# Channel loop of a gated attention and state-space kernel: the state recurrences of two neighbouring blocks overlapped by half

## The chip, the cores and the metric

The kernel runs on one core of one Trainium2 chip. The metric is the device time of one execution in microseconds (us); lower is better. The kernel before takes 2762.11 us (median of 3 runs, 2752.1 to 2769.66).

## The reference, cut to what matters

The reference computes a gated mix of two branches over a sequence of 2048 positions and 576 channels, and the gradients of it for twelve inputs. Branch A is multi-head attention with 32 heads of 18. Branch B is a state-space convolution with 128 complex states per channel:

```
logdA = dt * (A_re + 1j*A_im);  dB = dt * (B_re + 1j*B_im)
P = exp(logdA[:, :, None] * l)                  # channels x 128 states x 2048
K = einsum("dn,dnl,dn->dl", Cc, P, dB).real     # one filter of 2048 taps per channel
y = irfft(rfft(u) * rfft(K))[:L] + u * Dskip    # a causal convolution per channel
out = g * a + (1 - g) * b
```

The kernel does not form the filter. It cuts the sequence into 16 blocks of 128 positions (NB) and carries the 128 complex states of a channel from block to block: a recurrence of the form H[k] = Z * H[k-1] + U[k], with the complex number Z a constant of channel and state. The forward pass (call it h, s = 0 in the code) and the gradient (g, s = 1) are the same recurrence on two inputs, so a channel has four real rows: real and imaginary part of h and of g. There are NS = 15 states in sequence, that is one start value and 14 steps.

## The kernel before, in words

Three stages follow one another. Attention and its gradient take the first 2107 us or so. The channel loop is next, and it is the stage that changes. A last stage forms the weight gradients and the two outputs.

The channel loop goes over 18 blocks of 32 channels (NBLK = 18, CB = 32). The 128 states lie on the partitions. The work of block b is spread over several iterations, and these helpers do it:

- `load_en(b, h)` (L671) loads half h of the block's basis, E1n, 1 MB, from device memory. Six halves fit, so block b takes the place of block b-3, after `ybp(b-3, h)` has read it. `turn_e` (L654) transposes one half on TensorE (32 matmuls, etp) and copies it out on ScalarE (4 copies, E1e, L665).
- `m_load(b)` (L603) loads xs, 1 MB, and gyp; `m_part` (L610) multiplies them on TensorE (psM, 16 matmuls per call), copies the sum on ScalarE (mst, L620) and stores it (Md_d). `m_skw` (L628) reads Md_d back along a skewed pattern in four loads (skw), and `m_sum` and `m_fin` turn that into two more columns of RX.
- `prep_rx` (L590) makes the matmul input RX in three ScalarE instructions (L597 to L599), from RXn, which `load_rx` loads for two blocks at a time.
- `uv(b, h)` (L676) makes the inputs of the recurrence for half h: 32 matmuls (uvp) and 4 ScalarE evictions (UV, L690).
- `scan(b, 0, 15)` (L692) is the recurrence, on VectorE. A step is two chains, h and g, each of three instructions: a product of the last state with Z and with its swapped partner (tz, L704, 128x128), the addition of the input (L706, 128x64), and the sum of both products (HG, L708, 128x64). The chains alternate, so an instruction never depends on the one right before it.
- `casts` (L710), on ScalarE, makes bf16 copies hR and gR of the states. `rw1` and `rw2` (L719, L726), on VectorE, weight the states for the output. `ybp` (L756) multiplies them with E1n on TensorE (64 matmuls). `pairs1` and `pairs2` (L786, L793) multiply states with inputs on VectorE (pq, L774 and L802), and TensorE sums them (59 matmuls, misc); `sums` copies the sums out (m, L808).
- `k0(b)` (L732) computes tap 0 of the block's filter in 65 narrow matmuls, copies it (K0c, L744) and stores it; `t0_load` (L813) then loads T0w, 1 MB, the Toeplitz block made of the stored taps, and `t0` multiplies with it (32 matmuls).

The order is written out by hand for TensorE, ScalarE, VectorE and GpSimd: each engine runs its instructions in program order. Only the order of DMA issues on SyncE inside the loop is left to the framework's scheduler. All loads and stores of the loop are issued by SyncE into one hardware queue. The PSUM tiles etp, uvp and psM share one ring of four banks (tag "bk").

Of one iteration i before, this is the order: `k0(i+1)`, `uv(i+1, 0)`, `turn_e(i+1, 1)`, `scan(i)`, `casts(i)`, `rw1`, `rw2`, `t0(i)`, `uv(i+1, 1)`, `prep_rx(i+2)`, `ybp(i)`, `pairs1(i)`, `load_en(i+3)`, `turn_e(i+2, 0)`, `m_sum` and `m_fin(i+2)`, `pairs2(i)`, `sums(i)`, `m_part(i+3)`. So what block i+2 needs from the first half of its basis is made at the end of iteration i, and the rest in iteration i+1, beside the recurrence of block i.

Of the kernel before, what the change touches and what calls it, by code (L numbers as in the profile page):

```python
# [9 lines left out]
A = mybir.AluOpType  # L10
ACT = mybir.ActivationFunctionType
BF = mybir.dt.bfloat16
F32 = mybir.dt.float32
# [7 lines left out]
def build(tc, aps, dbg_aps=None, stages=("s1", "attn", "post", "s4", "final")):  # L21
# [40 lines left out]
    with ExitStack() as gctx:  # L62
# [538 lines left out]
        xss = {}  # L601

        def m_load(b, dma=nc.sync.dma_start):  # L603
            xs = xss[b] = Q["pl"].tile([P, NSUB, SUB, CB], BF, tag="xs", bufs=2, name="xs")
            src = bass.AP(tensor=xb_d.tensor, offset=xb_d[b:b + 1, 0:1, 0:1].offset,
                          ap=[[XR * SUB * CB, NB], [SUB * CB, NSUB], [1, NSUB * SUB * CB]])
            dma(xs.rearrange("p e t c -> p (e t c)"), src)
            dma(Q["gyp2"][b % 2][:, 0:SUB, :].rearrange("p t c -> p (t c)"), gyb_d[b])
# [56 lines left out]
                copy(E_[:, 4 * q:4 * q + 4], pt_)  # L665

        def load_par(b, dma=nc.sync.dma_start):
            par = blk(b)["par"] = Q["pw"].tile([P, 8, CB], F32, tag="par", bufs=2, name="par")
            dma(par, par_d[:, 0:8, b * CB:(b + 1) * CB])

        def load_en(b, h, dma=nc.sync.dma_start):  # L671
            dG = b * CB + h * GS
# [3 lines left out]
        def uv(b, h):  # L676
            B_ = blk(b)
            if h == 0:
                B_["UV"] = Q["pw"].tile([P, 2, NCOL, CB], BF, tag="UV", bufs=2, name="UV")
            UV = B_["UV"]  # L680
            E_ = B_["E"].pop(h)
            RX = RXs[b // 2][1]
            off = (b % 2) * CB + h * GS
            for q in range(2):
                for ri in range(2):
                    pr = Q["ps"].tile([P, NCOL, 8], F32, tag="bk", bufs=4, name="uvp")
                    for c_ in range(8):
                        mm(pr[:, :, c_], lhsT=E_[:, q * 8 + c_, ri, :], rhs=RX[:, off + q * 8 + c_, :])
                    c0 = h * GS + q * 8
                    nc.scalar.mul(UV[:, ri, :, c0:c0 + 8], pr, -1.0 if ri == 0 else 1.0)  # L690

        def scan(b, k0, k1):  # L692
            B_ = blk(b)
            UVk = B_["UV"][:, :, 0:2 * NB, :].rearrange("p r (s k) c -> p r s k c", s=2)
            if k0 == 0:
                B_["HG"] = Q["pw"].tile([P, 4, NS, CB], F32, tag="HG", name="HG")
                nc.vector.tensor_copy(B_["HG"][:, :, 0, :].rearrange("p (r s) c -> p r s c", s=2), UVk[:, :, :, 0, :])
                k0 = 1
            HG = B_["HG"].rearrange("p (r s) k c -> p s r k c", s=2)
            ZZ = B_["par"][:, 0:4, :].rearrange("p (m r) c -> p m r c", m=2)  # L700
            for k in range(k0, k1):
                tz = [Q["pw"].tile([P, 2, 2, CB], F32, tag=f"tz{s_}", bufs=2, name="tz") for s_ in range(2)]
                for s_ in range(2):
                    nc.vector.tensor_tensor(tz[s_], HG[:, s_, :, k - 1, :].unsqueeze(1).to_broadcast([P, 2, 2, CB]), ZZ, op=A.mult)  # L704
                for s_ in range(2):
                    nc.vector.tensor_tensor(tz[s_][:, 0], tz[s_][:, 0], UVk[:, :, s_, k, :], op=A.add)  # L706
                for s_ in range(2):
                    nc.vector.tensor_tensor(HG[:, s_, :, k, :], tz[s_][:, 0], tz[s_][:, 1, ::-1], op=A.add)  # L708

        def casts(b):  # L710
            B_ = blk(b)
# [6 lines left out]

        def rw1(b):  # L719
            B_ = blk(b)  # L720
            for nm, r_, tg in (("wa", 4, "wA"), ("wb", 5, "wB")):
                B_[nm] = Q["pw"].tile([P, 4 * NS, CB], F32, tag=tg, name=nm)
                nc.vector.tensor_tensor(B_[nm], B_["HG"].rearrange("p q k c -> p (q k) c"),
                                        B_["par"][:, r_, :].unsqueeze(1).to_broadcast([P, 4 * NS, CB]), op=A.mult)
# [7 lines left out]
        def k0(b):  # L732

            B_ = blk(b)
            wk = Q["pw"].tile([P, 2, CB], BF, tag="wk", bufs=2, name="wk")
            nc.scalar.copy(wk, B_["par"][:, 6:8, :])
            kps = Q["misc2"][b % 2][:, 13 * CB:14 * CB]
            mm(kps, lhsT=ident_bf[0:1, :], rhs=Q["dsk_row"][:, b * CB:(b + 1) * CB], start=True, stop=False)
            for ch in range(CB):
                for ri in range(2):  # L740
                    mm(kps[:, ch:ch + 1], lhsT=B_["En"][ch // GS][:, ch % GS, ri, :], rhs=wk[:, ri, ch:ch + 1],
                       start=False, stop=(ch == CB - 1 and ri == 1))
            K0c = Q["pw"].tile([P, CB], BF, tag="K0c", bufs=2, name="K0c")
            nc.scalar.copy(K0c, kps)  # L744
            nc.sync.dma_start(Kp_d[b, P:2 * P, :], K0c)
# [67 lines left out]
        def t0_load(b):  # L813
            B_ = blk(b)
            if "T0w" in B_:
                return
            T0w = B_["T0w"] = Q["pw"].tile([P, P, CB], BF, tag="T0w", bufs=2, name="T0w")
            src = bass.AP(tensor=Kp_d.tensor, offset=Kp_d[b:b + 1, 1:2, 0:1].offset, ap=[[CB, P], [1, P * CB]])
            nc.sync.dma_start(T0w.rearrange("p j c -> p (j c)"), src)

# [476 lines left out]
        if "s4" in stages:  # L1297
# [8 lines left out]
            with ExitStack() as ctx:  # L1306
# [24 lines left out]

                ctx.enter_context(tc.manual_schedule(engines={mybir.EngineType.PE, mybir.EngineType.Activation, mybir.EngineType.DVE, mybir.EngineType.Pool}))
                dve_copy = nc.vector.tensor_copy
                with tc.manual_schedule(engines={mybir.EngineType.SP}):
                    load_par(0)
                    prep_rx(0, dve_copy)
                    turn_e(0, 0, 0, 4, dve_copy)
                    m_sum(0)
                    m_fin(0)
                    uv(0, 0)  # L1340
                    turn_e(0, 1, 0, 4, dve_copy)
                    uv(0, 1)
                    m_skw(1)
                    load_en(2, 0)
                    load_par(1)
                    prep_rx(1)
                    k0(0)
                    t0_load(0)
                    turn_e(1, 0, 0, 4)
                    m_load(2)  # L1350
                    m_sum(1)
                    m_fin(1)
                    load_en(2, 1)
                for i in range(NBLK):
                    cur = True
                    nx = i + 1 < NBLK
                    mb = i + 3 if i + 3 < NBLK else None
                    sb = i + 2 if i + 2 < NBLK else None
                    if sb is not None and i > 0:
                        m_skw(sb)  # L1360
                    if sb is not None:
                        load_par(sb)
                    if mb is not None:
                        m_load(mb)
                    if sb is not None and sb % 2 == 0:
                        load_rx(sb // 2)
                    if nx and cur:
                        k0(i + 1)
                    if nx:
                        uv(i + 1, 0)  # L1370
                        turn_e(i + 1, 1, 0, 4)
                    if cur:
                        scan(i, 0, 15)
                        casts(i)
                        rw1(i)
                        rw2(i)
                        t0(i, 0)
                        t0(i, 1)
                    if nx:
                        uv(i + 1, 1)  # L1380
                    if sb is not None:
                        prep_rx(sb)
                    if i == 0:
                        m_part(2, 0)
                        m_part(2, 1)
                        m_skw(2)
                    if cur:
                        if nx:
                            t0_load(i + 1)
                        ybp(i, 0)  # L1390
                        ybp(i, 1)
                        pairs1(i)
                    if cur and mb is not None:
                        load_en(mb, 0)
                        load_en(mb, 1)
                    if sb is not None:
                        turn_e(sb, 0, 0, 4)
                        m_sum(sb)
                        m_fin(sb)
                    if cur:  # L1400
                        pairs2(i)
                        sums(i)
                    if mb is not None:
                        m_part(mb, 0)
                        m_part(mb, 1)
                    if cur:
                        BK.pop(i)

        while rights:
            rights.pop().__exit__(None, None, None)  # L1410
# [295 lines left out]
```

## Time and profile before

| what | value |
|---|---|
| median of 3 runs | 2762.11 us (2752.1 to 2769.66) |
| the profiled execution | 2755.74 us, its span 2754.0 us |
| TensorE / VectorE / ScalarE busy over the span | 88% / 85% / 86% |
| mean granted TensorE clock | 0.954 |
| first instruction of the first recurrence (HG, L697) | 2119.04 us |
| last sum of the last block on TensorE ends | 2584.50 us |
| recurrence instructions (L704, L706, L708) | 3 x 504 |

The shares over the whole span say little about the loop, since attention fills three quarters of it. The loop is read from the stretch 2119 to 2585 us: the busy time of each engine in windows of 50 us, the groups of instructions there, and one iteration of about 25 us in order of time. A start-to-start distance of two instructions on one engine is what an instruction costs in a queue; its listed duration is longer, since the end of one overlaps the start of the next.

### The profile page before, as it was taken

How to read it: one execution, taken by the hardware profiler on the slowest of the kernel's cores; microseconds unless marked ns; L12 is line 12 of the kernel's file. 1: busy time of each engine (PE TensorE's matmuls, PEld its weight loads, DVE VectorE, ACT ScalarE, POOL GpSimd, SP SyncE). 2: the span in 40 equal slices, each digit the busy share in tenths (PEclk: the TensorE clock that was granted, in tenths of full speed). 3: DMA queues.
4: the chain of work that ended last, by engine and by line, in shares of the span. 5: the costliest groups of instructions: out<-in, count | busy, mean ns of one | idle time of the engine just before them, and what ended most of it. 6: DMA issues, size and time to landing. Idle time of an engine off the chain costs nothing.

```text
span 2754.0 us, 70696 instructions
## 1 busy us (share of the span) xinstructions
PE 2429.9 (88%) x27411; PEld 1170.9 (43%) x27411; DVE 2348.6 (85%) x4850; ACT 2368.6 (86%) x2749; POOL 1611.9 (59%) x2667
## 2 busy tenths in 40 slices
PE   8798989988989988889999889988885899999789
PEld 4433333333333333333333333333323788888557
DVE  5649999999999998899999989998985899999954
ACT  5489999999999999999999999999974788888221
POOL 0278878888988888788888878888501000000010
PEclk9889999999999999999999999999977899899899
DMA  7637899889888978987997898797779898986995
GB/s 226 182 102 157 150 169 179 160 159 190 158 159 175 173 159 165 176 161 157 175 161 163 160 172 162 152 186 151 138 156 204 228 257 219 246 238 167 254 244 137
DMA packets 1256763, 490.81 MB, mean 178 GB/s; under 512 B 1151781, under 2 KB 1228182, under 8 KB 1247210
## 3 DMA queue, kind: packets, MB, share of 16 engines
q1 hardware_dynamic: 1219946, 413.78, 73.2%
q0 software_dynamic: 23120, 59.76, 8.8%
q10 hardware_dynamic: 13360, 12.75, 1.6%
q8 instruction: 214, 3.51, 0.5%
q14 instruction: 123, 1.01, 0.1%
HBM read 145.68 MB, written 98.52 MB: 89 GB/s over the span
## 4 chain that ended last, share of the span: by engine, by line
ACT 38%; PE 26%; DVE 23%; issue 6%; DMA 4%; POOL 2%; SPq 1%; ACTq 0%; DVEq 0%; POOLq 0%
ACT eb L1271 22%; ACT PT L1266 14%; DVE ds L1276 7%; PE ps_P L30 7%; DVE tz L704 3%; PE accV L30 2%; PE ps_dx L30 2%; PE turn_p L988 2%; DVE tz L706 2%; DVE HG L708 2%; PE accK L30 1%; PE ps_dwq L30 1%; DVE pq L774 1%; PE misc L30 1%; DMA dsT<-ds 1%
## 5 line engine op out<-in xcount | busy, mean ns | idle before, releaser
L1276 DVE TENSOR_TENSOR ds<-ps_P,PT 128x512 bf16<-128x512 f32 x2048 | 1312.6, 684 | 135.2 <-PE ps_P L30 97.5
L1271 ACT ACTIVATE eb<-ps_P 128x1024 bf16<-128x1024 f32 x1024 | 1100.8, 1075 | 31.1 <-PE ps_P L30 31.1
L1266 ACT ACTIVATE PT<-ps_P 128x1024 bf16<-128x1024 f32 x1024 | 1105.8, 1081 | 20.9 <-PE ps_P L30 19.6
L30 PE MATMUL ps_P<-dOaT,VaT_g 32*128 32x512 bf16 x2048 | 580.9, 388 | 31.1 <-DVE ds L1276 15.6
L502 POOL TENSOR_TENSOR et<-eG,eT 128x448 f32<-128x448 f32 x576 | 542.2, 961 | 10.7
L30 PE MATMUL ps_P<-QaT_g,KaT_g 32*128 32x512 bf16 x2048 | 402.0, 385 | 137.3 <-ACT PT L1266 122.8
L30 PE MATMUL ps_P<-KaT_g,QaT_g 32*128 32x512 bf16 x2048 | 406.1, 389 | 2.5 <-ACT eb L1271 1.9
L30 PEld LDWEIGHTS <-KaT_g 32*128 32x128 bf16 x2048 | 147.6, 91 | 467.3 <-issue 451.3
L502 POOL TENSOR_TENSOR Eo<-et,et 128x448 bf16<-128x448 f32 x288 | 326.9, 1135 | 20.7
L810 POOL TENSOR_TENSOR SS<-m 128x96 f32<-128x96 f32 x18 | 9.7, 537 | 429.5 <-ACT m L808 384.5
L30 PEld LDWEIGHTS <-QaT_g 32*128 32x128 bf16 x2048 | 116.0, 91 | 286.3 <-issue 263.9
L30 PE MATMUL accV<-eb,dOa 128*32 128x512 bf16 x2048 | 184.5, 393 | 27.5 <-ACT eb L1271 27.2
L30 PE MATMUL accO<-PT,Vtok_g 128*32 128x512 bf16 x2048 | 206.9, 393 | 0.1
L30 PE MATMUL accK<-dsT,Qtok_g 128*32 128x256 bf16 x4096 | 163.0, 280 | 14.8 <-DMA dsT<-ds 13.0
L30 PE MATMUL accQ<-ds,Ktok_g 128*32 128x512 bf16 x2048 | 160.3, 391 | 2.3 <-DVE dvacc L1042 2.2
L30 PEld LDWEIGHTS <-Vtok_g 128*32 128x32 bf16 x2048 | 52.7, 93 | 222.0 <-issue 222.0
L993 DVE COPY dsT<-turn_p 128x1024 bf16<-128x1024 bf16 (+1 forms) x216 | 139.3, 645 | 2.3 <-PE turn_p L988 2.3
L988 PE MATMUL turn_p<-ident_bf,ds 128*128 128x128 bf16 x1664 | 133.8, 223 | 1.6 <-DVE gb L1060 0.8
L665 ACT COPY E1e<-etp 128x1024 bf16<-128x1024 bf16 x136 | 128.8, 1060 | 3.4 <-PE etp L664 3.3
L704 DVE TENSOR_TENSOR tz<-HG,par 128x128 f32<-128x128 f32 x504 | 126.7, 295 | 0.6
L502 POOL TENSOR_TENSOR et<-eT 128x32 f32<-128x32 f32 (+3 forms) x288 | 115.8, 422 | 11.4
L30 PEld LDWEIGHTS <-Qtok_g 128*32 128x32 bf16 x4096 | 88.4, 97 | 77.7 <-issue 60.5
(264 smaller groups left out, 3692.5 us busy)
## 6 DMA issues: line engine op xcount, KB each, us to landing
E_d<-Eo POOLq DMA_DIRECT2D x144, 256.0 KB, 3.3
E1n<-E_d SPq DMA_DIRECT2D x36, 1024.0 KB
xs<-xb_d SPq DMA_DIRECT2D x18, 1024.0 KB
T0w<-Kp_d SPq DMA_DIRECT2D x18, 1024.0 KB
Md_d<-mst SPq DMA_DIRECT2D x36, 288.0 KB
dsT<-ds SPq DMA_TRANSPOSE x512
dqkv_d<-dtk POOLq DMA_DIRECT2D x96, 72.0 KB, 4.3
skw<-Md_d SPq DMA_DIRECT2D x72, 64.0 KB
```

Of the source, the lines that this page charges most:

```text
L30: return nc.tensor.matmul(out, lhsT=lhsT, rhs=rhs, start=start, stop=stop, **kw)
L502: nc.gpsimd.tensor_tensor(out, a, b, op=op)
L665: copy(E_[:, 4 * q:4 * q + 4], pt_)
L704: nc.vector.tensor_tensor(tz[s_], HG[:, s_, :, k - 1, :].unsqueeze(1).to_broadcast([P, 2, 2, CB]), ZZ, op=A.mult)
L706: nc.vector.tensor_tensor(tz[s_][:, 0], tz[s_][:, 0], UVk[:, :, s_, k, :], op=A.add)
L708: nc.vector.tensor_tensor(HG[:, s_, :, k, :], tz[s_][:, 0], tz[s_][:, 1, ::-1], op=A.add)
L774: nc.vector.tensor_tensor(o.rearrange("p a b n c -> p a b (n c)"), a_.rearrange("p b n c -> p b (n c)").unsqueeze(1).to_broadcast([P, 2, 2 ...
L988: nc.tensor.transpose(pt_[:, x, qb, :], t_[:, qb * P:(qb + 1) * P], ident_bf)
L993: (nc.scalar.copy if NTOT <= now[0] < NTOT + OFF else nc.vector.tensor_copy)(o_(), pt_[:, x:x + n])
L1266: nc.scalar.activation(U["PT"][i, j // 2], ps, ACT.Exp)
L1271: nc.scalar.activation(e, ps, ACT.Exp)
L1276: nc.vector.tensor_tensor(U["ds"][i][:, j, :], ps, U["PT"][i, j // 2][:, j % 2, :], op=A.mult)
```

## The change

The recurrence of block i+1 is started half an iteration before that of block i is done. KH = 8. In iteration i one call of `scan` runs steps 8 to 14 of block i and steps 1 to 7 of block i+1 as two alternating chains. A chain now handles h and g together: its instructions are twice as wide (tz 128x256, the additions and sums 128x128), and there are half as many. Only the first half of block 0 (ahead of the loop) and the second half of block 17 still split h from g.

For that, Z has to lie in the parameters twice, so `load_par` issues three DMAs in place of one and reads four of the eight rows twice. UV(i+2) must be complete one iteration earlier than before. So in iteration i both `turn_e` and both `uv` of block i+2 are done, and `m_part(i+3)`, `m_skw(i+3)`, `prep_rx(i+3)` come ahead of `ybp(i)`. `t0` stands first in an iteration, then `k0(i+1)`. The loop before the first iteration grows by the work that moved forward.

Buffers: UV gets three and HG two; xs and T0w, 1 MB each, have one instead of two.

```diff
@@ -601,7 +601,7 @@
         xss = {}
 
         def m_load(b, dma=nc.sync.dma_start):
-            xs = xss[b] = Q["pl"].tile([P, NSUB, SUB, CB], BF, tag="xs", bufs=2, name="xs")
+            xs = xss[b] = Q["pl"].tile([P, NSUB, SUB, CB], BF, tag="xs", bufs=1, name="xs")
             src = bass.AP(tensor=xb_d.tensor, offset=xb_d[b:b + 1, 0:1, 0:1].offset,
                           ap=[[XR * SUB * CB, NB], [SUB * CB, NSUB], [1, NSUB * SUB * CB]])
             dma(xs.rearrange("p e t c -> p (e t c)"), src)
@@ -665,8 +665,10 @@
                 copy(E_[:, 4 * q:4 * q + 4], pt_)
 
         def load_par(b, dma=nc.sync.dma_start):
-            par = blk(b)["par"] = Q["pw"].tile([P, 8, CB], F32, tag="par", bufs=2, name="par")
-            dma(par, par_d[:, 0:8, b * CB:(b + 1) * CB])
+            par = blk(b)["par"] = Q["pw"].tile([P, 12, CB], F32, tag="par", bufs=2, name="par")
+            for s_ in range(2):
+                dma(par[:, s_:8:2, :], par_d[:, 0:4, b * CB:(b + 1) * CB])
+            dma(par[:, 8:12, :], par_d[:, 4:8, b * CB:(b + 1) * CB])
 
         def load_en(b, h, dma=nc.sync.dma_start):
             dG = b * CB + h * GS
@@ -676,7 +678,7 @@
         def uv(b, h):
             B_ = blk(b)
             if h == 0:
-                B_["UV"] = Q["pw"].tile([P, 2, NCOL, CB], BF, tag="UV", bufs=2, name="UV")
+                B_["UV"] = Q["pw"].tile([P, 2, NCOL, CB], BF, tag="UV", bufs=3, name="UV")
             UV = B_["UV"]
             E_ = B_["E"].pop(h)
             RX = RXs[b // 2][1]
@@ -689,23 +691,36 @@
                     c0 = h * GS + q * 8
                     nc.scalar.mul(UV[:, ri, :, c0:c0 + 8], pr, -1.0 if ri == 0 else 1.0)
 
-        def scan(b, k0, k1):
+        def scan_open(b):
             B_ = blk(b)
-            UVk = B_["UV"][:, :, 0:2 * NB, :].rearrange("p r (s k) c -> p r s k c", s=2)
-            if k0 == 0:
-                B_["HG"] = Q["pw"].tile([P, 4, NS, CB], F32, tag="HG", name="HG")
-                nc.vector.tensor_copy(B_["HG"][:, :, 0, :].rearrange("p (r s) c -> p r s c", s=2), UVk[:, :, :, 0, :])
-                k0 = 1
-            HG = B_["HG"].rearrange("p (r s) k c -> p s r k c", s=2)
-            ZZ = B_["par"][:, 0:4, :].rearrange("p (m r) c -> p m r c", m=2)
-            for k in range(k0, k1):
-                tz = [Q["pw"].tile([P, 2, 2, CB], F32, tag=f"tz{s_}", bufs=2, name="tz") for s_ in range(2)]
-                for s_ in range(2):
-                    nc.vector.tensor_tensor(tz[s_], HG[:, s_, :, k - 1, :].unsqueeze(1).to_broadcast([P, 2, 2, CB]), ZZ, op=A.mult)
-                for s_ in range(2):
-                    nc.vector.tensor_tensor(tz[s_][:, 0], tz[s_][:, 0], UVk[:, :, s_, k, :], op=A.add)
-                for s_ in range(2):
-                    nc.vector.tensor_tensor(HG[:, s_, :, k, :], tz[s_][:, 0], tz[s_][:, 1, ::-1], op=A.add)
+            HG = B_["HG"] = Q["pw"].tile([P, 4, NS, CB], F32, tag="HG", bufs=2, name="HG")
+            UVk = B_["UVk"] = B_["UV"][:, :, 0:2 * NB, :].rearrange("p r (s k) c -> p r s k c", s=2)
+            nc.vector.tensor_copy(HG[:, :, 0, :].rearrange("p (r s) c -> p r s c", s=2), UVk[:, :, :, 0, :])
+
+        def scan(*chains):
+
+            def part(b, s_):
+                B_ = blk(b)
+                HG, ZZ = B_["HG"], B_["par"][:, 0:8, :].rearrange("p (m q) c -> p m q c", m=2)
+                if s_ is None:
+                    return HG, ZZ, B_["UVk"], 4
+                return HG[:, s_::2], ZZ[:, :, s_::2], B_["UVk"][:, :, s_:s_ + 1], 2
+
+            todo_ = []
+            for x, (b, k0, k1, s_) in enumerate(chains):
+                todo_.append((x, part(b, s_), k0, k1))
+            for t in range(max(k1 - k0 for _, _, k0, k1 in todo_)):
+                live = [(x, p_, k0 + t) for x, p_, k0, k1 in todo_ if k0 + t < k1]
+                tz = {}
+                for x, (HG, ZZ, UVk, n), k in live:
+                    tz[x] = Q["pw"].tile([P, 2, 4, CB], F32, tag=f"tz{x}", bufs=2, name="tz")[:, :, 0:n]
+                    nc.vector.tensor_tensor(tz[x], HG[:, :, k - 1, :].unsqueeze(1).to_broadcast([P, 2, n, CB]), ZZ, op=A.mult)
+                for x, (HG, ZZ, UVk, n), k in live:
+                    t0v = tz[x][:, 0].rearrange("p (r s) c -> p r s c", r=2)
+                    nc.vector.tensor_tensor(t0v, t0v, UVk[:, :, :, k, :], op=A.add)
+                for x, (HG, ZZ, UVk, n), k in live:
+                    t0v, t1v = [tz[x][:, m].rearrange("p (r s) c -> p r s c", r=2) for m in range(2)]
+                    nc.vector.tensor_tensor(HG[:, :, k, :].rearrange("p (r s) c -> p r s c", r=2), t0v, t1v[:, ::-1], op=A.add)
 
         def casts(b):
             B_ = blk(b)
@@ -814,7 +829,7 @@
             B_ = blk(b)
             if "T0w" in B_:
                 return
-            T0w = B_["T0w"] = Q["pw"].tile([P, P, CB], BF, tag="T0w", bufs=2, name="T0w")
+            T0w = B_["T0w"] = Q["pw"].tile([P, P, CB], BF, tag="T0w", bufs=1, name="T0w")
             src = bass.AP(tensor=Kp_d.tensor, offset=Kp_d[b:b + 1, 1:2, 0:1].offset, ap=[[CB, P], [1, P * CB]])
             nc.sync.dma_start(T0w.rearrange("p j c -> p (j c)"), src)
 
@@ -1331,6 +1346,7 @@
 
                 ctx.enter_context(tc.manual_schedule(engines={mybir.EngineType.PE, mybir.EngineType.Activation, mybir.EngineType.DVE, mybir.EngineType.Pool}))
                 dve_copy = nc.vector.tensor_copy
+                KH = NS // 2 + 1
                 with tc.manual_schedule(engines={mybir.EngineType.SP}):
                     load_par(0)
                     prep_rx(0, dve_copy)
@@ -1341,70 +1357,72 @@
                     turn_e(0, 1, 0, 4, dve_copy)
                     uv(0, 1)
                     m_skw(1)
-                    load_en(2, 0)
+                    m_load(2)
                     load_par(1)
                     prep_rx(1)
+                    scan_open(0)
+                    scan((0, 1, KH, 0), (0, 1, KH, 1))
+                    load_rx(1)
+                    turn_e(1, 0, 0, 4)
+                    m_sum(1)
+                    m_fin(1)
+                    uv(1, 0)
+                    load_en(2, 0)
                     k0(0)
                     t0_load(0)
-                    turn_e(1, 0, 0, 4)
-                    m_load(2)
-                    m_sum(1)
-                    m_fin(1)
+                    turn_e(1, 1, 0, 4)
+                    m_part(2, 0)
+                    m_part(2, 1)
+                    uv(1, 1)
                     load_en(2, 1)
+                    m_skw(2)
+                    m_load(3)
+                    prep_rx(2)
                 for i in range(NBLK):
-                    cur = True
                     nx = i + 1 < NBLK
                     mb = i + 3 if i + 3 < NBLK else None
                     sb = i + 2 if i + 2 < NBLK else None
-                    if sb is not None and i > 0:
-                        m_skw(sb)
-                    if sb is not None:
-                        load_par(sb)
-                    if mb is not None:
-                        m_load(mb)
-                    if sb is not None and sb % 2 == 0:
-                        load_rx(sb // 2)
-                    if nx and cur:
+                    if mb is not None and mb % 2 == 0:
+                        load_rx(mb // 2)
+                    if nx:
+                        scan_open(i + 1)
+                        scan((i, KH, NS, None), (i + 1, 1, KH, None))
+                    else:
+                        scan((i, KH, NS, 0), (i, KH, NS, 1))
+                    t0(i, 0)
+                    t0(i, 1)
+                    if nx:
                         k0(i + 1)
-                    if nx:
-                        uv(i + 1, 0)
-                        turn_e(i + 1, 1, 0, 4)
-                    if cur:
-                        scan(i, 0, 15)
-                        casts(i)
-                        rw1(i)
-                        rw2(i)
-                        t0(i, 0)
-                        t0(i, 1)
-                    if nx:
-                        uv(i + 1, 1)
-                    if sb is not None:
-                        prep_rx(sb)
-                    if i == 0:
-                        m_part(2, 0)
-                        m_part(2, 1)
-                        m_skw(2)
-                    if cur:
-                        if nx:
-                            t0_load(i + 1)
-                        ybp(i, 0)
-                        ybp(i, 1)
-                        pairs1(i)
-                    if cur and mb is not None:
-                        load_en(mb, 0)
-                        load_en(mb, 1)
+                        t0_load(i + 1)
                     if sb is not None:
                         turn_e(sb, 0, 0, 4)
                         m_sum(sb)
                         m_fin(sb)
-                    if cur:
-                        pairs2(i)
-                        sums(i)
+                        uv(sb, 0)
+                        turn_e(sb, 1, 0, 4)
+                    casts(i)
+                    rw1(i)
+                    rw2(i)
+                    if sb is not None:
+                        load_par(sb)
+                        uv(sb, 1)
                     if mb is not None:
                         m_part(mb, 0)
                         m_part(mb, 1)
-                    if cur:
-                        BK.pop(i)
+                        m_skw(mb)
+                    if mb is not None and mb + 1 < NBLK:
+                        m_load(mb + 1)
+                    if mb is not None:
+                        prep_rx(mb)
+                    ybp(i, 0)
+                    ybp(i, 1)
+                    pairs1(i)
+                    if mb is not None:
+                        load_en(mb, 0)
+                        load_en(mb, 1)
+                    pairs2(i)
+                    sums(i)
+                    BK.pop(i)

         while rights:
             rights.pop().__exit__(None, None, None)
```

In `rw1` and `k0` the row numbers of the parameters change to fit (4, 5 become 8, 9; 6:8 becomes 10:12); nothing else there changes.

More of the change, by code (lines that the diff above doesn't have):

```diff
@@ L720, in rw1 @@
             B_ = blk(b)
-            for nm, r_, tg in (("wa", 4, "wA"), ("wb", 5, "wB")):
+            for nm, r_, tg in (("wa", 8, "wA"), ("wb", 9, "wB")):
                 B_[nm] = Q["pw"].tile([P, 4 * NS, CB], F32, tag=tg, name=nm)
@@ L735, in k0 @@
             wk = Q["pw"].tile([P, 2, CB], BF, tag="wk", bufs=2, name="wk")
-            nc.scalar.copy(wk, B_["par"][:, 6:8, :])
+            nc.scalar.copy(wk, B_["par"][:, 10:12, :])
             kps = Q["misc2"][b % 2][:, 13 * CB:14 * CB]
```

## The prediction

> **What bounds the kernel now.** I read the profile page first, then the windows over the channel loop, then one iteration per engine in order of time. Windows of 50 us (busy us of each engine, granted TensorE clock, DMA share, GB/s):
>
> ```profile
> core 0: us, PE busy (x) PEld busy (x) DVE busy (x) ACT busy (x) POOL busy (x), PEclk, DMA share, GB/s
> 2300.00:2350.00 50.00, 46.37 (x781) 44.03 (x779) 49.45 (x189) 42.94 (x66) 1.70 (x4) 0.90 0.90 236
> 2350.00:2400.00 50.00, 45.41 (x757) 43.06 (x754) 49.45 (x189) 41.12 (x64) 1.66 (x4) 0.86 0.91 236
> ```
>
> VectorE is busy 49.45 of 50 us: it bounds the loop. Its timeline starts recurrences at 2431.60 and 2456.60, a period of 25.0 us. But nothing else is idle: TensorE 23.2, ScalarE 21.4, DMA 0.9 x 25 = 22.6 us per iteration. So a shorter VectorE period is only gained if all of these keep up, in an order that lets them.
>
> VectorE in order of time, one step of the recurrence and what follows the last:
>
> ```profile
> 2456.86 0.50 DVE L704 TENSOR_TENSOR tz<-HG,par 128x128 f32<-128x128 f32 x2
> 2457.27 0.35 DVE L706 TENSOR_TENSOR tz<-tz,UV 128x64 f32<-128x64 f32 x2
> 2457.54 0.36 DVE L708 TENSOR_TENSOR HG<-tz 128x64 f32<-128x64 f32 x2
> 2457.81 0.49 DVE L704 TENSOR_TENSOR tz<-HG,par 128x128 f32<-128x128 f32 x2
> ```
>
> From start to start a product of 128 elements costs 0.41/2 = 0.20 us, an addition of 64 costs 0.27/2 = 0.135. A step is 0.95 us, 14 steps 13.2 of the 25.0.
>
> ScalarE and TensorE in the same iteration, pieces I need below:
>
> ```profile
> 2445.38 3.76 ACT L665 COPY E1e<-etp 128x1024 bf16<-128x1024 bf16 x4
> 2449.00 1.02 ACT L715 CAST hR<-HG 128x960 bf16<-128x960 f32 x1
> 2449.89 1.02 ACT L715 CAST gR<-HG 128x960 bf16<-128x960 f32 x1
> 2450.79 0.33 ACT L717 COPY CK<-UV 128x128 bf16<-128x128 bf16 x1
> 2450.99 2.09 ACT L690 ACTIVATE UV<-uvp 128x512 bf16<-128x512 f32 x4
> ```
>
> Start to start: four E1e cost 3.62, the casts 2.0, four UV 1.9 us.
>
> And SyncE's queue, the line of DMA issues that the loop rests on:
>
> ```profile
> 2463.84 0.55 SPq L607 DMA_DIRECT2D xs<-xb_d  x1
> 2464.49 1.09 SPq L621 DMA_DIRECT2D Md_d<-mst  x2
> 2466.73 0.33 SPq L745 DMA_DIRECT2D Kp_d<-K0c  x1
> 2467.11 0.59 SPq L608 DMA_DIRECT2D gyp<-gyb_d  x1
> 2472.95 2.54 SPq L634 DMA_DIRECT2D skw<-Md_d  x4
> ```
>
> The skew loads must wait until Md_d has landed. They issue 9.1 us after xs, although DMA was idle when xs was issued (16 GB/s in 2463.5 to 2464.5): 1 MB and 2 x 288 KB stand in front. This costs nothing now, since skw has most of an iteration.
>
> **What the Trainium skill says.** (1) "Vector Engine (DVE) Microarchitecture Reference", Measured stream behaviour: 1.04 ns per column plus about 75 ns per instruction. The trace agrees: 0.135 and 0.20 us for 64 and 128 elements give 1.06 ns and 67 ns. (2) "DMA: Bandwidth & Descriptors", Queues, rings and completion order: the DMAs that SyncE issues share one ring on each DMA engine, consumed in ring order. The trace agrees with the wait above. (3) "TensorE: Matmul & The Clock Gate", Part 1: the clock halves after about 3.4 us of little work and recovers after as much work. The trace shows it: 0.50 in 2441.5 to 2444.5, just behind the narrow matmuls of `k0`, where UV evictions are 0.83 apart instead of 0.5.
>
> **The change, part by part.**
>
> *Recurrence.* A wide product costs 256 x 1.06 + 67 = 0.34 us, wide additions and sums 0.20 each. One round of two chains: 2 x (0.34 + 0.20 + 0.20) = 1.48; seven rounds 10.4 us for 13.2. Dependent instructions stand at least 0.4 us apart against a product's 0.43 us duration and an addition's 0.30 (duration is about elements/0.96 GHz + 0.16), so no stall. VectorE's own sum falls to 25.0 - 2.8 = 22.2 us.
>
> *Order of ScalarE and TensorE.* This is what I expect to decide. Both run in program order and hand over to each other through the four "bk" banks. In the new order nearly everything is one ring: `ybp(i)` 3.37, `pairs` sums 0.86 + 2.55, `t0(i+1)` 1.97, `k0(i+2)` 1.63, first quarter of etp 0.45, four E1e 3.62, `m_fin` 0.45, first quarter of uvp 0.45, four UV 1.9, four E1e 3.62, casts 2.0, first UV of the second half 0.5 (it frees the bank that psM needs), `m_part` 2.07, then `ybp(i+1)`. With four handovers of 0.2 (psM to mst, uvp to UV in the trace) the ring is 26.2 us, already above 25.0. Before, `turn_e(i+2,0)`, `m_part` and both `uv` stood apart, so that ScalarE's `prep_rx` (4.3) and TensorE's sums ran beside each other; now ScalarE does `prep_rx` while TensorE goes through ybp, sums, t0 and k0, and then waits for K0c.
>
> *Loads.* SyncE's order in the changed program repeats every two iterations. After the psM that frees the only xs buffer: xs, Md_d x2, then for odd i yd, skw x4, E1n x2; for even i E1n, skw x4, E1n. E1n(i+3) needs the buffer that `ybp(i)` reads, as before; but `turn_e(i+3, 0)` now comes in iteration i+1 right after `k0`, 3.4 + 2.0 + 1.6 us and half of ybp behind that release, not an iteration later. Cost, from the end of psM to E1n landed. Odd: handover 0.2; xs issue to skw issue 9.1 less 0.6 for the gyp that stood between (128 KB at the 220 GB/s of that stretch) = 8.5; four skw issues 2.55; E1n issue 0.6, its 1 MB at 300 to 404 GB/s (404 in 2458.5 to 2461.5, the pair took 7 us) 3.0, start and landing 0.8. Sum 15.6. Even: 0.2 + 0.6 + 0.3, data of xs and Md_d 7.3, E1n 3.0, landing 0.5: 11.9. From there back to the end of psM: 0.45 + 3.62 + 0.45 + 0.45 + 1.9 + 3.62 + 2.0 + 0.5 + 2.07 + 0.8 = 15.9. Periods 31.5 and 27.8, mean 29.7. The PE idle this leaves ahead of etp (5.2 us for odd i) should halve the clock behind it: slower m_sum (+0.9) and UV spacing (+1.3) in part of the odd iterations, 0.4 on the mean. I take 30.1 us.
>
> *Hidden parts.* T0w waits behind par, which waits for `rw1b(i)` (15 us into VectorE's iteration); it lands some 7 us later, before the late t0. Two more par issues (0.43 each) and 512 small packets: hidden likewise, about 1 us of DMA if not. UV and HG buffers cost nothing but room. Behind the waiting etp stand m_sum, uv, psM, ybp on TensorE and everything on ScalarE; VectorE waits for hR and for UV(i+2).
>
> *The sum.* Iteration 0 can start when UV(1) is complete. On ScalarE from 2118.89: RX 3.9, E1e 3.6, m_fin 0.45, UV 1.9, wk to K0c 2.3, E1e 3.6, mst 1.0, UV 1.9, handovers 1.4: 2139. `prep_rx(2)`, wk, k0, K0c bring the first E1e to 2145.6, and the ring from there (15.2) the first psM to 2160.8. Fourteen periods of 30.1: 2582. Then 11.9 and 15.0 to UV(17), iteration 16 on VectorE 10.4 + 6.6 + 4.5, the last half recurrence 6.65, weights 6.6, ybp 3.4, sums 3.4: 2650. Before, this point is 2584.5: +66 us on 2755.7, hence 2822 us. The profiled time lies 6.4 us below the median of the runs (2762.11), inside their spread, so I leave it.
>
> **Rivals.**
> - *Only the ring decides*, the DMAs land in time (shared rings that move faster than in the stretch above). Period 26.2: 2160.8 + 14 x 26.2 + 10.4 + 15.0 + 41.6 = 2595, +10: 2766 us. For: the 404 GB/s that E1n reaches. Against: the 9.1 us measured on an idle queue.
> - *VectorE still bounds, and the change is faster.* Period 22.2, place: recurrence to recurrence on VectorE. 2139 + 17 x 22.2 + 20 = 2536, -48: 2707 us. It decides if ring and loads both fit below 22.2, and the kernel is faster from a period of about 25.5 down. For: each engine's own busy sum is below 23.2. Against: the ring's parts are measured and leave 4 us too many.
> - *Clock halved for most of each ring*: psM +1.5, UV +1.3 in every period, about +2.6: 14 x 2.6 = +36: 2858 us.
> - *The wide instructions are not cheaper* (no row of that shape before: from 13.2, if cost went by element at two accesses, to 10.4). I take 10.4; either end is hidden when VectorE no longer bounds, so this moves nothing but the faster rival.
>
> **How the numbers follow.** Loads and ring together 0.55 (2790 to 2850), ring alone 0.22 (2755 to 2790), halved clock 0.15 (2850 to 2885), VectorE bound 0.08 (2700 to 2755). Range for 8 in 10: 2760 to 2866, cutting the faster case and the upper end of the clock case. A measurement here tells about 1% from no change: faster than 2734.5: 0.06; within 1%: 0.2; slower: 0.74.
>
> **What would show it.** VectorE's share in the loop near 22.2/30 = 0.74, with waits for hR and UV; E1e or etp preceded by idle of about 5 and 1.5 us in turn, put down to E1n's DMA; skw issued 8 to 9 us after xs; recurrence starts alternating near 31 and 28 us apart; a granted clock below 0.90. I am wrong if recurrences start 25 us apart or less with VectorE at 0.99, or if etp never waits (then the ring alone).

## The result, and the profile after

The changed kernel takes 2891.76 us (median of 4 runs, 2886.86 to 2905.44), the kernel before beside it 2759.70 us (4 runs). The ratio is 1.048, 95% interval 1.043 to 1.054: slower by 4.8%. The predicted sign holds, but the time lies above the range of 2760 to 2866. The profiled execution took 2886.86 us, with a span of 2885.1 us, against a span of 2754.0 us before: 131 us to account for.

First the windows over the loop of the changed kernel (busy us of each engine, granted TensorE clock, DMA share, GB/s), the same stretches as before:

```profile
core 0: us, PE busy (x) PEld busy (x) DVE busy (x) ACT busy (x) POOL busy (x), PEclk, DMA share, GB/s
2300.00:2350.00 50.00, 35.33 (x519) 33.03 (x516) 28.83 (x59) 31.43 (x49) 9.10 (x4) 0.76 0.74 189
2350.00:2400.00 50.00, 37.52 (x652) 34.77 (x652) 40.26 (x102) 31.89 (x49) 12.20 (x4) 0.83 0.72 177
```

No engine is full any more, and neither is DMA. VectorE was busy 49.45 of 50 us, now 28.83 and 40.26; over 2220 to 2540 us it is 213.59 of 320, 0.67. With nothing full, the time is in waits. Three lines of those of 2200 to 2600 us name the circle (engine and line, releaser, us in total, times, longest):

```profile
DVE pq L789 <- ACT hR L730: 134.4, 12, 15.4
ACT E1e L665 <- PE etp L664: 78.3, 15, 8.8
PE etp L664 <- DMA E1n<-E_d: 66.0, 13, 7.9
```

Read from the bottom: TensorE waits for the basis, ScalarE for TensorE, VectorE for ScalarE. The circle closes because the loads of the next basis are issued only behind psM, which itself comes 16 to 19 us behind etp. Recurrences start 30.5 and 35.1 us apart in turn (means of seven periods each, from the third start on; 32.8 together) instead of 25.0.

Three stretches make up the 131 us, each read from the first start of a recurrence and the last sum of `sums`' matmuls in the two traces:

| stretch | before | after | difference |
|---|---|---|---|
| up to the first HG copy | 2119.04 | 2110.95 | -8 |
| from there to the last sum | 465.5 | 577.8 | +112 |
| from the last sum to the end | 169.5 | 196.4 | +27 |

The first lies within the spread of attention's end (first HG copies come at 2107 to 2122 us in the profiles of nine of the kernels below). The second was predicted in kind. The third was not predicted at all. It shows in SyncE's queue and on TensorE at the end of the loop, before and then after:

```profile
2554.18 0.39 SPq L1433 DMA_DIRECT2D x_tok_b<-in_A_x_dram  x1
2555.86 19.66 SPq L1450 DMA_DIRECT2D dq_all<-dqkv_d  x4
```

```profile
2584.34 5.92 PE L30 MATMUL ps_dwq<-dq_all,x_tok_b 128*128 128x426 bf16 x32
```

```profile
2690.34 0.39 SPq L1451 DMA_DIRECT2D x_tok_b<-in_A_x_dram  x1
2690.82 8.89 SPq L1468 DMA_DIRECT2D dq_all<-dqkv_d  x2
```

```profile
2705.81 1.58 PE L30 MATMUL ps_dwq<-dq_all,x_tok_b 128*128 128x426 bf16 x4 [17.10 <-DMA dq_all<-dqkv_d]
```

Before, the last stage's first inputs were issued 30 us ahead of the loop's last sum (2584.5), and its first matmul started there. After, they are issued 1.6 us behind it (2688.7), and TensorE stands for 17.1 us. Nothing in the diff mentions these loads. Among SyncE's own waits, the load of x_tok_b (L1451) stands for 36.8 us, until the last store of yd has landed:

```profile
SPq L1451 <- DMA yd_d<-yd: 36.8, 1, 36.8
```

What ties the two together is x_tok_b's place in SBUF. In the program's memory map it has bytes 153568 to 172000 of each partition, in both kernels. The working tiles at lower addresses grew: UV by 8192 bytes, HG by 7680, tz by 2048, par by 1024, while T0w shrank by 8192, in all 10752. So yd, which begins at 139936 and takes 4096 bytes, moved to 150688, and m4 from 144032 to 154784, into x_tok_b's bytes. Both are in use until behind the loop's last sum: GpSimd reads m4 until 2690.1.

### The profile page after: what moved, and what is told of

Its sections match the earlier page's. It is cut to its first block, busy times and chain, and to the rows that moved or that the text cites. A ratio compares the mean times of both kernels' runs of the same rounds, so it can differ in the third digit from the quotient of the medians.

```text
span 2885.1 us, 70053 instructions
## 1 busy us (share of the span) xinstructions
PE 2456.6 (85%) x27411; PEld 1191.1 (41%) x27411; DVE 2295.9 (80%) x4136; ACT 2369.4 (82%) x2749; POOL 1697.4 (59%) x2667
## 5 line engine op out<-in xcount | busy, mean ns | idle before, releaser
L825 POOL TENSOR_TENSOR SS<-m 128x96 f32<-128x96 f32 x18 | 66.7, 3704 | 475.0 <-ACT m L823 421.4
L789 DVE TENSOR_TENSOR pq<-UV,hR 128x1920 bf16<-128x1920 bf16 x36 | 40.1, 1155 | 166.1 <-ACT hR L730 165.9
L664 PE MATMUL etp<-ident_bf,E1n 128*128 128x128 bf16 x1152 | 102.0, 269 | 68.1 <-DMA E1n<-E_d 68.1
L664 PEld LDWEIGHTS <-E1n 128*128 128x128 bf16 x1152 | 95.7, 126 | 69.7 <-DMA E1n<-E_d 69.3
```

The costliest lines, as they stand in the source:

```text
L664: nc.tensor.transpose(pt_[:, c_, ri, :], En[:, 4 * q + c_, ri, :], ident_bf)
L789: nc.vector.tensor_tensor(o.rearrange("p a b n c -> p a b (n c)"), a_.rearrange("p b n c -> p b (n c)").unsqueeze(1).to_broadcast([P, 2, 2 ...
L825: nc.gpsimd.tensor_tensor(o_[:, :, 0], m4[:, :, 0], m4[:, :, 3], op=A.subtract)
```

## The experiments

My theory after the traces: (A) the loop's period is the time in which E1n lands and, behind it, that of the TensorE-ScalarE ring from etp to the end of psM; (B) the last stage is late because of x_tok_b's bytes. Rivals: the ring alone; the halved clock; a last stage that is longer for other reasons. All ratios are to the kernel before on the same chip.

**e1_t0w_last**, for (B). One edit puts an early tile behind the late ones:

```
-  T0w = B_["T0w"] = Q["pw"].tile( ...
+  T0w = B_["T0w"] = Q["ple"].tile( ...
```

> The changed kernel with one edit: the T0w buffer is taken from the pool behind the working pool, so that yd, m4 and E1e move down by 8 KB and x_tok_b's bytes lie only over E1e and T0w, which are last used 20 us before the loop ends. Theory (last stage delayed by buffers): the loop keeps its period of 32.8 us, x_tok_b is issued near 2671 instead of 2690, the first ps_dwq matmul comes 12 to 16 us earlier, and the kernel takes 2877 us, between 2872 and 2882 (1.041 to 1.045 of before). Rival (the last stage is longer for another reason, as bandwidth): time unchanged, 2886 to 2896, x_tok_b may be earlier but ps_dwq is not.

Measured 2872.42 us, 1.043 (1.039 to 1.048). The interval overlaps that of the changed kernel, so the traces have to decide. The loop keeps its period (32.6 us). The first load of the last stage with SyncE's wait for it, and the first matmul, in this kernel, whose last sum ends at 2690.6:

```profile
2674.83 0.39 SPq L1451 DMA_DIRECT2D x_tok_b<-in_A_x_dram  x1
```

```profile
SPq L1451 <- PE yp L30: 14.5, 1, 14.5
```

```profile
2691.50 0.70 PE L30 MATMUL ps_dwq<-dq_all,x_tok_b 128*128 128x426 bf16 x3 [0.90 <-DMA dq_all<-dqkv_d]
```

The load comes 16 us ahead of the last sum instead of behind it, the wait falls from 17.1 to 0.9 us, and the stretch behind the loop from 196.4 to 180.8 us. It repeats: the four kernels with T0w in this place (this one, e6, e8 and e9) take 181 to 184 us behind the loop, the changed kernel and its five other variants 196 to 206. The rest of the way to 169.5 is not given back. T0w, which now holds those bytes, is itself read by the last block's `t0` (the yp matmuls that the load waits for); that all of the other 11 us come from this is not shown.

**e5_before_late_bytes**, the same cause put into the kernel before:

```
-  ydx[b // 2] = Q["pw"].tile( ...
+  ydx[b // 2] = Q["ple"].tile( ...
-  m4 = Q["pw"].tile( ...
+  m4 = Q["ple"].tile( ...
```

> The kernel before with one edit: m4 and yd are taken from the pool behind the working pool, so that they lie in the bytes of x_tok_b, as they do in the changed kernel. Nothing else moves in the loop. Theory (the last stage's prefetch is lost when a late tile lies in x_tok_b's bytes): period 25.0 as before, x_tok_b issued within 8 us of the last sum's end or behind it instead of 30 us ahead, ps_dwq starts 15 to 22 us after the last sum, and the kernel takes 2780 us, 2772 to 2788 (1.005 to 1.010 of before). Rival (the prefetch was worth nothing, the last stage is bound elsewhere): 2755 to 2764.

Measured 2801.47 us, 1.017 (1.015 to 1.019), 43 us for an edit that moves no instruction: twice what I expected. The period stays 25.0. The stretch behind the loop becomes 195.6 us (+26). The load comes 3.5 us behind the last sum (2601.5), and TensorE stands as in the changed kernel:

```profile
2605.03 0.38 SPq L1433 DMA_DIRECT2D x_tok_b<-in_A_x_dram  x1
```

```profile
2620.36 1.94 PE L30 MATMUL ps_dwq<-dq_all,x_tok_b 128*128 128x426 bf16 x5 [18.86 <-DMA dq_all<-dqkv_d]
```

The other 17 us stand ahead of the loop. The first HG copy comes at 2135.7 instead of 2119.0, because the first copy of the basis on VectorE waits:

```profile
2126.70 1.89 DVE L665 COPY E1e<-etp 128x1024 bf16<-128x1024 bf16 x3 [13.87 <-DMA dqkv_d<-dtk]
```

My edit let E1e slide down to byte 139936, over attention's dtk (144736 to 145312 in the map), whose store must finish first. In the kernel before, E1e began at 145568, just above it. So the same mechanism works at both ends of the loop, and (B) is shown in both directions.

**e2_en_first**, for (A): only SyncE's order in the loop changes, written out by hand.

```
     m_part(mb)                        # Md_d x2
     ...
-    m_skw(mb); m_load(mb + 1)         # E1n behind, by the scheduler
     ybp(i, 0)
+    load_en(mb, 0); m_skw(mb)
     ybp(i, 1)
+    load_en(mb, 1); m_load(mb + 1); yd_store(i)
```

> The changed kernel with another order of SyncE's loads in the loop, everything else kept: behind Md_d come E1n(0), skw, E1n(1), and only then gyp, xs and yd. Theory (E1n's landing behind xs, Md_d and skw sets the period): the wait of etp for E1n falls from 4.9 us on the mean to below 1.5, the period from 32.8 to 26.2 to 28.5 us, and the kernel takes 2815 us, 2798 to 2832 (1.014 to 1.026 of before). Rival (the ring of TensorE and ScalarE in program order sets the period, the loads only fill its slack): period above 31, 2870 to 2895.

Measured 2820.91 us, 1.023 (1.021 to 1.026). SyncE's issues behind psM, and what TensorE then does:

```profile
2390.28 1.21 SPq L621 DMA_DIRECT2D Md_d<-mst  x2
2392.27 0.33 SPq L676 DMA_DIRECT2D E1n<-E_d  x1
2392.74 4.36 SPq L634 DMA_DIRECT2D skw<-Md_d  x4
2397.20 0.40 SPq L676 DMA_DIRECT2D E1n<-E_d  x1
2397.64 0.56 SPq L607 DMA_DIRECT2D xs<-xb_d  x1
```

```profile
2400.35 0.64 PE L30 MATMUL misc<-wk,E1n 128*128 128x1 bf16 x20
2400.85 0.91 PE L664 MATMUL etp<-ident_bf,E1n 128*128 128x128 bf16 x8
```

etp follows `k0` with no wait, in every iteration. From psM's end to etp it takes 10.4 us, and the periods are even, 27.6 us on the mean. The 1 MB of xs, now last, is not missed by psM: TensorE, ScalarE and VectorE wait for no DMA at all from 2160 to 2600 us.

**e3_no_en** takes the loads away altogether, so that blocks 3 to 17 are computed with the basis of blocks 0 to 2:

```
+  if b >= 3:
+      blk(b)["En"][h] = keep[b % 3, h]      # tile of an earlier block
+      return
   ...
```

> The changed kernel without the E1n loads of blocks 3 to 17: they reuse the tiles of blocks 0 to 2, so their outputs are computed from the wrong basis. It leaves out 30 loads of 1 MB and their waits. Theory (loads set the period, and below them the ring): the period falls to 26.2 us, what the ring alone costs, at most 27.5, and the kernel takes 2800 us, 2790 to 2820. Rival (half clock and ring alone): period stays above 30, 2850 or more. If the loads were the only bound and VectorE came next, the period would be 22.2 us and the time 2740 to 2750.

Measured 2824.45 us, 1.024 (1.022 to 1.027), period 27.9. Without 30 MB of traffic the kernel is no faster than with the loads in the right order. So bandwidth was not the limit, order was; and below the loads lies a ring of 27.6 to 27.9 us. I had put it at 26.2 and expected 2800.

**e4_warm** and **e7_wait_filled**, for the halved clock. Idle matmuls ahead of etp:

```
+  if i % 2:                # e4: 60;   e7: i % 2 == 0 and i > 0, 110
+      for _ in range(NW): mm(misc2[0][:, 14 * CB:16 * CB], lhsT=ident_bf, rhs=ident_bf[:, 0:2 * CB])
```

> The changed kernel with 60 idle matmuls of 64 columns ahead of turn_e(i+2, 0) in odd iterations, where TensorE waits 6 to 8 us for E1n; they write to unused columns and change nothing in the result. Theory (the idle wait halves the clock, and what comes behind it up to psM takes 18.6 us instead of 16.3): the odd iterations lose about 2 us, the kernel takes 2876 us, 2866 to 2884. Rival (TensorE's clock is off the path there, ScalarE's evictions set the pace): unchanged, 2886 to 2898. If the wait is shorter than the 60 matmuls it gets slower by the difference.

> As e4_warm, but with the idle matmuls (110 of 64 columns) in even iterations, ahead of the E1n wait that is 7 us long: in e4_warm they stood ahead of the short one, and cost up to their own 3.3 us. Theory (the wait halves the clock, and etp to psM then takes up to 18.7 us instead of 16.3): iterations with the long wait take 16.3 us from etp to psM, 0.9 us less on their mean, the kernel takes 2880 us, 2874 to 2886. Rival (the clock is halved by the narrow matmuls of t0, k0 and m_sum, not by the wait, since it is halved in e2 and e3 as well, where etp doesn't wait): 2886 to 2900, the spread of etp to psM remains.

e4 measured 2898.25 us, 1.051 (1.049 to 1.054). It missed its aim: the loads of an odd iteration are waited for in the next, even one, so the matmuls stood ahead of the short wait. e7 puts them ahead of the long wait and measured 2901.55 us, 1.052 (1.051 to 1.054), not faster either. The matmuls fill some 4.9 us of it, and TensorE's wait for E1n falls from 66.0 to 38.0 us in the same 400 us, but the period is 33.2. From etp to psM's end it takes 17.1 us on the mean instead of 17.3, still between 16.2 and 18.6. Filling most of the long wait does not help; the case without any wait ahead of etp is e2, where the stretch takes 17.2.

**e10_no_k0** asks whether the run of single-column matmuls does it (on top of e2; two of 64 stay):

```
-  for ch in range(CB):
+  for ch in (CB - 1,):
```

> e2_en_first with 2 of the 64 single-column matmuls of k0: 62 products of each block's K0 are left out, so part of the outputs is wrong. Their 1.7 us go out of the ring in any case. Theory A (the run of single-column matmuls halves the clock for what follows): etp to the end of psM, 16.2 to 18.1 us and 17.2 on the mean in e2, becomes 16.3 everywhere, the period 27.6 - 1.7 - 0.9 = 25.0, the kernel 2785 us, 2780 to 2791. Theory B (something else halves it, as t0's or m_sum's short matmuls or the pauses for ScalarE): mean stays near 17.2, period 25.9, 2797 us, 2792 to 2803.

Measured 2789.31 us, 1.014 (1.011 to 1.017). The time is in the range of this expectation's theory A, but 3.6 us of the gain are in the first two periods (22.4 and 24.3 become 19.8 and 23.3), which neither theory counted; the period of the loop, 25.9, is that of its theory B. From etp to psM's end it takes 16.7 us on the mean instead of 17.2, mostly near 16.0 or near 17.1. The narrow matmuls have a part in it: without them the clock is full over the first 4 us behind etp in 13 of 14 iterations, in e2 in 4 of 15. But in each of these 13 it is halved at a later place of the stretch. So `k0` is at most a part of the cause of the halving, and the rest stays open. Where the halving lies, windows of e2 show, around one `k0` that ends at 2427.7 and is followed by etp with no wait:

```profile
2424.00:2427.00 3.00, 3.00 (x74) 2.93 (x73) 3.00 (x13) 0.62 (x2) 2.41 (x1) 1.00 0.97 295
2427.00:2430.00 3.00, 3.00 (x59) 3.00 (x56) 3.00 (x7) 1.92 (x3) 3.00 (x2) 0.72 1.11 270
2430.00:2432.00 2.00, 2.00 (x13) 2.00 (x12) 2.00 (x2) 2.00 (x3) 0.75 (x1) 0.50 0.96 197
2436.00:2438.00 2.00, 2.00 (x22) 2.00 (x20) 0.00 (x0) 1.49 (x3) 0.00 (x0) 0.50 0.35 42
2440.00:2442.00 2.00, 1.28 (x18) 1.03 (x17) 0.18 (x1) 2.00 (x3) 0.00 (x0) 1.00 0.80 269
```

TensorE counts as busy throughout the first three, and the clock (the third column from the right) falls to 0.50 all the same, and stays there until 2438; the first pause, of 0.6 us, comes at 2432. The Trainium skill's "TensorE: Matmul & The Clock Gate" (Part 1), which the prediction names, tells of halving behind an idle window of about 3.4 us. Here the measurement decides: a pause in the records is not needed. The place that the prediction cites, 0.50 from 2441.5 in the kernel before, says the same: in the 3.4 us ahead of it TensorE paused for 0.8 us at most.

**e6_en_first_t0w_last** puts both repairs together.

> The two edits together: E1n ahead of xs in SyncE's order, and T0w behind the other working tiles. Theory (the two costs are separate: one is in the loop's period, one behind the loop): the savings of 70 and 14 us add, 2807 us, 2800 to 2814. Rival (they share a cause): 2815 to 2822.

Measured 2808.21 us, 1.018 (1.016 to 1.020): the two costs add, as expected. In its profile 504.3 - 465.5 = 39 us remain in the loop and 14 behind it.

**e8_reordered** and **e9_casts_early** ask whether the overlap pays once the order lets it. e8, with T0w last, moves `m_part` and `k0` to the head and `t0` behind etp:

```
   scan(i / i+1)
+  m_part(mb); k0(i + 1)
   turn_e(sb, 0)
+  t0(i); t0_load(i + 1)
   m_sum(sb); m_fin(sb); m_skw(mb); uv(sb, 0); turn_e(sb, 1); casts(i); rw(i)
   load_par(sb); m_load(mb + 1); uv(sb, 1); prep_rx(mb); ybp(i) ... pairs(i)
```

> The wide alternating recurrence in another order of TensorE, ScalarE and SyncE, with T0w behind the other tiles: m_part and k0 lead the iteration, t0 stands behind turn_e(i+2, 0), prep_rx runs beside uv and ybp; SyncE takes Kp, Md, T0w, skw, par, gyp, xs, E1n(0), yd or RXn, E1n(1). All work is kept. Theory (what remains of the period after E1n is early, 27.6 us, is the ring of TensorE and ScalarE, and moving t0 and m_part out of it shortens it by about 3): period 24.5 to 26.0, the kernel takes 2775 us, 2757 to 2795 (1.00 to 1.013 of before). Rival (VectorE's own pace or DMA bandwidth already holds 27.6): 2800 to 2812, no gain over e6. A time below 2750 would mean the overlap pays once the order lets it.

> e8_reordered with three further moves: the casts hR and gR stand on ScalarE behind the first E1e instead of behind the second (ScalarE waited 1.5 us there for m_sum, and VectorE 4.8 us for hR), wk is made at the end of the iteration before (k0 waited 0.8 us for it), and ahead of the loop xs(3) is loaded before skw(2) and E1n(2,1) (the first psM of the loop waited 12.6 us for it). Theory (in e8 the ring of TensorE, 26.0 us, still sets the period): period 24.5 to 25.5, the second iteration 7 us shorter, 2770 us, 2756 to 2784 (0.999 to 1.009 of before). Rival (half clock and DMA hold 26.0): 2784 to 2795. Below 2745 the overlap would have paid.

e8 measured 2791.53 us, 1.012 (1.010 to 1.014), period 26.0; e9 2782.39 us, 1.012 (1.008 to 1.015; the kernel before had 2753.73 beside it), period 25.5, loop 474.1 us. With TensorE's order changed and nothing left out, the period falls by 1.6 and 2.1 us below e2's. T0w's new place leaves it as it was (e6: 27.6), and in e2 no wait for a load stood in it any more, so it was the order of TensorE and ScalarE that held it there. VectorE's largest wait in e9 (2200 to 2540 us) has changed its place:

```profile
DVE HG L706 <- ACT UV L700: 48.0, 13, 4.4
```

It now waits 3.7 us per iteration for the state inputs, 22 us of work in 25.5. None of these kernels beats the one before, and I have no version that does.

## Why the prediction was wrong in size

Right: VectorE no longer bounds, and its own sum per iteration is 0.667 x 32.8 = 21.9 us (predicted 22.2); the seven double rounds take 10.36 us (10.4). The circle is the one named. skw issues 8.7 us behind xs in the iteration below, as worked out. Periods alternate, VectorE waits for hR, and the clock in the loop is 0.80. The bound was read rightly because each handover was costed from a row.

The rows that show the size of the load step for an odd iteration, SyncE and then TensorE of the changed kernel (psM ends at 2450.5):

```profile
2450.54 0.57 SPq L607 DMA_DIRECT2D xs<-xb_d  x1
2451.20 1.09 SPq L621 DMA_DIRECT2D Md_d<-mst  x2
2456.41 0.57 SPq L786 DMA_DIRECT2D yd_d<-yd  x1
2459.28 3.94 SPq L634 DMA_DIRECT2D skw<-Md_d  x4
2463.31 0.88 SPq L676 DMA_DIRECT2D E1n<-E_d  x2
```

```profile
2468.38 0.93 PE L664 MATMUL etp<-ident_bf,E1n 128*128 128x128 bf16 x7 [7.33 <-DMA E1n<-E_d]
```

| term | predicted | measured |
|---|---|---|
| psM's end to etp, long / short (mean of 7 / 6) | 15.6 / 11.9 | 17.9 / 13.4 |
| etp to psM's end | 15.9, +0.4 for the clock | 17.3 (16.0 at full clock, in e4) |
| mean period | 30.1 | 32.8 |
| first psM's end | 2160.8 | 2157.7 |
| 14 periods | 421.4 | 459.2 |
| last psM to last sum | 68 | 71.8 |
| last sum to the end | 169.5, unchanged | 196.4 |

The step that failed outright is "UV and HG buffers cost nothing but room", with the last stage taken over unchanged in the sum. Room was just what cost something: +27 us, two fifths of the 65 by which 2822 is too low. Experiments e1 and e5 show it. Nothing in the rivals held it, since all of them lay in the loop.

The other 38 us are terms of the right mechanism with the wrong size, 14 x 2.7: 1.8 us per period are the waits for the loads, 0.9 the clock. Of the long wait's 2.3 us, 1.4 are the issue of the four skew loads in this iteration, 3.94 us instead of the 2.55 copied from the kernel before; in the seven long waits it takes 2.8 to 5.3 us, 4.3 on the mean. From E1n's issue to etp it takes 5.1 us instead of 4.4. The 1.5 us of the short wait are not taken apart here.

The half clock, which I put at 0.4 us per period and tied to the idle time ahead of etp, costs 1.3 on the mean. That is measured against one iteration of e4, which runs at full clock from etp to psM's end and takes 15.96 us, the 15.9 of the sum:

```profile
2433.80:2449.76 15.96, 11.14 (x170) 9.63 (x171) 8.36 (x8) 14.30 (x23) 0.40 (x1) 1.00 0.71 189
```

In the changed kernel the clock is low in the first 4 us behind etp every time, and the time follows what comes next. Eight of 14 iterations take 16.4 to 16.7 us and have a clock of 0.98 or more from 4 to 8 us behind etp's start; the other six take 17.9 to 18.7 and have 0.50 there. One of each, with 16.36 and 18.65 us:

```profile
2208.84:2212.84 4.00, 3.31 (x54) 3.23 (x54) 0.00 (x0) 3.26 (x9) 0.00 (x0) 1.00 0.59 238
2406.25:2410.25 4.00, 3.42 (x28) 3.35 (x29) 0.00 (x0) 2.29 (x6) 0.00 (x0) 0.50 0.59 240
```

The idle time is not what tells them apart: behind the long wait and behind the short one the mean is 17.3, and without a wait, in e2 and e3, it is 17.2 and 17.4. So the rival "clock halved for most of each ring" had half of its 2.6 us, with a wait or without one.

The rival "only the ring decides" is refuted for the changed kernel by e2 (5.2 us per period are the loads' order). Its number, 26.2, was also 1.4 to 1.7 too low, as e2 and e3 measure. Nearly all of that is the clock again: the rest of the ring, from psM's end to etp, takes 10.4 us in e2, just what its parts add up to. That VectorE would bound at 22.2 is refuted by the trace, and even in e9 it still waits.

One term came out by luck. The first psM's end, 2157.7 for 2160.8, looks well met, but the loop began 8.1 us earlier than in the profile from which it was reckoned; the way from the first HG copy to it took 46.8 us instead of 41.8.

## What to carry to other kernels

A longer prefetch distance is paid in buffers, and here the buffers shifted every tile behind them: look up which late tile comes to lie under the next stage's first load, and which early one under the previous stage's last store. When an engine with 25 us of work per iteration is relieved by 3 us while TensorE, ScalarE and DMA have 21 to 23, ask first whether their order can still close in that time, and put the load that the circle waits for first in its queue. Take the price of a DMA issue from a queue as full as it will be: the four skew loads took 2.55 us before and 4.3 on the mean in the long waits after.

## What the runs showed beside that

The first of GpSimd's two additions in `sums` (SS, 128x96) takes 385 ns at the least, but 3860 ns in the median of the changed kernel (453 before), up to 7706; the second takes 2297 in the median (406 before), about as long as one weighting on VectorE. They now run beside the recurrence and `rw1` there. The Trainium skill's "SBUF — State Buffer" (section "SBUF: two separate sides") says that a VectorE instruction with two SBUF inputs and a GpSimd one that reads SBUF exclude each other for the whole instruction; the trace agrees with that in kind, by these times. The weightings on VectorE beside them take 2.34 us instead of 2.16. I found neither on the path that sets the period.

An edit of memory placement alone, with no instruction added or moved, cost 1.7% (e5).
